# A fused attention and rational-MLP kernel: softmax sums of five early units on TensorE, fourteen rounded copies on ScalarE, a new order for the first 31 steps, and a last store in two halves

## The chip, the core and the metric

One core of one Trainium2 chip runs one program. The metric is device time in microseconds (us), the median over runs; a profiled execution gives the span, from the first to the last instruction, and a trace of every instruction. TensorE is written PE (its matmuls) and PEld (its weight loads), VectorE is DVE, ScalarE is ACT, GpSimd is POOL, and SyncE (SP) issues the transfers.

## The reference, cut to what matters

```
for c in range(seq // 32):                      # attention over chunks of 32 queries
    k_full, v_full = [mem (8 keys), k or v from 16 before to 8 after the chunk]
    scores = q_c @ k_full.T / 8
    a = exp(scores - max(scores)); a = a / (sum(a) + 1e-9)
    out_c = a @ v_full
x = out as 3072 tokens x 512                     # 4 batches x 768 tokens, 8 heads x 64
h = x @ w_in                                     # 512 x 2048
P = a0 + a1*h + a2*h**2 + a3*h**3
Q = 1 + |b0|*|h| + |b1|*h**2
y = (P / (Q + 1e-6)) @ w_out                     # 2048 x 512
```

The weights come as 64-bit floats; the kernel rebuilds each value from its two 32-bit words.

## The kernel before

**Blocks, units, steps.** The 3072 tokens are six blocks of 512. A block's attention is done in four *units* (i, p): block i, head pair p. The MLP is done in 96 *steps*, one for a block and one of 16 slices of 128 of the 2048 hidden columns. Every matrix of the MLP is split into a rounded high part and a low remainder, so that each product is three matmuls (high by high, high by low, low by high). A step n is: `g`, the first product (L477, 12 matmuls 128x512 into a PSUM bank `h`); a chain of eleven element-wise instructions on ACT, DVE and POOL; and `o`, the second product (L492, 12 matmuls into the four banks that hold a block's 512 output rows).

**The chain of a step**, with its letter: `s` |h| (L536, ACT), `S` slope (L541, ACT), `p` product for Q (L545, POOL), `i` line (L550, ACT), `j` and `J` the polynomial (L554 and L558, DVE), `t` and `T` logarithm and exponential for 1/Q (L565 and L569, ACT), `r`, `R`, `Q` ratio, error, mend (L573, L577, L581, DVE), `u` the rounded high part `ghi` (L586, POOL), `y` the low part `glo` (L593, POOL). There are two `h` banks, and 1/Q is kept in the step's own bank, so that step n+2's `g` can start only when step n's mend has read it.

**Units of blocks 0 and 1**, again with letters: `b` scores (L354, 16 matmuls 32x128), `m` and `M` maximum and subtraction (DVE), `x` exponential (ACT), `c` transposes on TensorE into a bank `ep` (L405), `k` copy of `ep` to `eT` (ACT), `d` values (L421, 16 matmuls with slices of `eT` as weights), `z` and `D` the softmax sums (DVE, L319 over 128x512 and L329), `G` reciprocal, `n` normalisation to `xt` (DVE, L432), `e` transposes back (L442), `h` and `l` high and low parts of x. Later units go through other functions.

**Weights** are converted in 32 halves, one `in` and one `out` half for each slice: `w` load, `A` (ACT, `stage`), `B` and `C` (DVE, L186 and L191), `H` high part (ACT, L198), `L` low part (POOL, L203).

**What sets the order.** `SEQ` is a list of such letters, worked off one by one; each engine keeps its instructions in that order, and SP its transfers. It holds the starting phase and the first 31 steps; `ORDER` says which weight half is converted next, `CLEAR` which engine clears which buffer at the start, `RAW_SLOTS` and `SPARE` which buffers hold raw words and spare rows. From step 31 on a loop writes the order, and `FINAL` the last steps. A capital `W` is a transpose that only keeps TensorE at work; `Y` loads the polynomial's constants `par`, and `P` takes |b| from them on ACT.

**The end.** `evac` (L525) copies each output bank through ACT to `v_main` and stores it, 256 KB for 128 rows.

Of the kernel before, what the change touches and what calls it, by code (L numbers as in the profile page):

```python
# [48 lines left out]
SEQ = """
w q00 b00 q02 A m00 q01 b02 v00 M00 m02 M02 x00 c00 q03 x02 W W b01 k00 B C W W d00 z00 D00 m01 b03 H v02 W c02 G00  # L50
M01 x01 k02 z02 m03 n00 D02 z01 w M03 d02 e00 q10 v01 A G02 c01 x03 n02 B k01 h00 C e02 b10 L l00 H D01 z03 h02 W W
d01 q11 D03 m10 c03 Y b11 M10 x10 G01 k03 v03 G03 n01 l02 z10 w e01 m11 w M11 D10 d03 h01 f00 n03 e03 w G10 A l01 B
h03 L f01 f02 x11 l03 A w f03 f10 C P q12 z11 B i f11 s j C c10 A f12 B H v10 D11 f13 S b12 A J C i L k10 w p B H t j
L C J G11 q13 T c11 m12 s d10 S r H n10 M12 R p e10 A L H t w B x12 T v11 Q w u C r b13 L h10 H l10 m13 L R k11 v12 g
M13 c12 A s i z12 w d11 Q B g j S p n11 J x13 k12 v13 C A t c13 D12 u T z13 d12 r G12 e11 k13 R H n12 s Q y D13 i d13
h11 B G13 w w e12 w C S g j A L H n13 A y B J p L h12 i t T w s l11 C S B w w H o j r l12 A R Q C u A J B H w o p B g
C u t y L T r s o R i Q S L p C g j A y A H H L B J t T w C o i r R Q s L j u S B J H C p A B t g y L T A o u s r C S
e13 R Q i j h13 p H J H l13 y B L L t g o T u C r R i Q j w J s S p A H B t g T y A C o r B R w Q s L i S C j A H H u
A J B p w w g y C t T r L i R s u S Q j o L g H J E0 p E1 B E2 t C y T L u E3 w r s R S Q w i j H p w A J t T B C o y
A r u R Q g w B o i s y L S H j A p u J t w g B y T L C C H s r R Q o i g S A p j J A H B B C o t T s r L L S i u R Q  # L60
H p A j y g J B t o T r C R s Q L i u j w S w g J H A y p o t B u C T r H w R Q i s L L A j S p J B C t g T y s i r u
R Q S y A j o C H p J g t v21 T L w B s u C y S H v20 r R o i Q p L H j u g A J A t B T B r R Q i C s L o S g j J y H
p C u t T r H o R L i Q s S L j q20 J g p y X t T o i b20 s r u j R Q J q21 m20 S p t T g M20 y i r u o R b21 x20 j s
Q S c20 w y p m21 J t M21 T g o s q22 r i z20 R x21 j d20 b22 u v22 S c21 Q J q23 D20 G20 z21 g y p o t T n20 D21 s S
r R Q u g i m22 j y o J p u G21 t T M22 x22 i r s R y j c22 S d21 b23 p Q J e20 z22 g t T o m23 r s i u S R Q M23 E0 j
E1 h20 J g n21 p t x23 y D22 T s v23 z23 S p c23 d22 r R E2 e21 Q u D23 G22 E3 i o K j y G23 g J n22 t u o q30 T r R
d23 i y l20 s Q S j h21 e22 J p g n23 t T r u s R Q o l21 y u y h22 S p g v30 i o e23 l22 j J i j t h23 T s r l23 R Q
J S o p g
# [749 lines left out]
```

## Time and profile before

| | us |
|---|---|
| median of 3 runs (lowest, highest) | 606.92 (604.62, 607.4) |
| profiled execution, its own time | 605.13 |
| its span | 603.0 |
| PE busy, of the span | 585.9 (97%) |
| DVE, ACT, POOL busy | 467.7, 396.7, 418.6 |

Busy is the time in which an engine had an instruction under way. For TensorE that says little, as matmuls overlap; how fast it can go is read where one product follows the other without a wait. What an engine waited for is in the view of waits, with the instruction that released it.

### The profile page before, as it was taken

The page shows a single profiled execution, that of the slowest core. Times are in us where ns is not written, and L with a number is a line of the kernel's source. Part 1 is how long each engine was busy: PE and PEld are TensorE (multiplying, and loading weights), DVE is VectorE, ACT ScalarE, POOL GpSimd, SP SyncE. Part 2 cuts the span into 40 slices and gives each one's busy share as a digit, 9 for nine tenths or more (in the row PEclk, how much of TensorE's full clock was granted, in tenths as well). Part 3 has the DMA queues.
Part 4 walks back from the last instruction along what each step waited for, and adds up shares of the span by engine and source line. Part 5 has one row for each costly group of instructions (what it writes and reads, how often), then busy time and mean ns, then how long its engine had stood idle before and what let it go on. Part 6 is the DMA issues. An engine that isn't in the chain of part 4 may idle for free.

```text
span 603.0 us, 12757 instructions
## 1 busy us (share of the span) xinstructions
PE 585.9 (97%) x4949; PEld 475.9 (79%) x4949; DVE 467.7 (78%) x765; ACT 396.7 (66%) x651; POOL 418.6 (69%) x388
## 2 busy tenths in 40 slices
PE   7879989999999999999999999999999999999997
PEld 6658767888778778878888888888888888888886
DVE  6999989988788758888778787787787776666673
ACT  4699879888557465565566665565756566756673
POOL 4369989999654875666685767667676767666682
PEclk9999999999999999999999999999999999999999
DMA  8968204630243704433313412312510100100001
GB/s 299 353 250 306 121 0 147 244 134 1 84 145 107 234 21 148 143 86 96 92 38 88 167 35 78 109 36 76 174 37 7 36 5 15 70 1 0 1 0 71
DMA packets 34588, 61.12 MB, mean 101 GB/s; under 512 B 4192, under 2 KB 20576, under 8 KB 34144
## 3 DMA queue, kind: packets, MB, share of 16 engines
q1 hardware_dynamic: 34528, 60.31, 30.6%
q8 instruction: 39, 0.64, 0.4%
q14 instruction: 21, 0.17, 0.1%
HBM read 44.57 MB, written 7.34 MB: 86 GB/s over the span
## 4 chain that ended last, share of the span: by engine, by line
PE 82%; DMA 5%; DVE 5%; POOL 4%; issue 2%; ACT 1%; SPq 1%; POOLq 0%; ACTq 0%; DVEq 0%
PE h L477 39%; PE o L492 38%; DMA w_raw<-in_w_dram 3%; PE pairs L312 2%; PE pairs L290 2%; POOL w_hl L203 1%; DMA v_main<-in_vm_dram 1%; DMA xf<-blocks 1%; POOL glo L593 1%; DMA qk_pairs<-in_qk_dram 1%; PE pa L421 1%; SPq L145 1%; DVE ct L558 0%; DVE ct L573 0%; DVE ct L581 0%
## 5 line engine op out<-in xcount | busy, mean ns | idle before, releaser
L477 PE MATMUL h<-x_hi,w_hl 128*128 128x512 f32 x768 | 240.6, 394 | 2.0 <-DVE ct L581 1.7
L492 PE MATMUL o<-w_hl,ghi 128*128 128x512 f32 x768 | 236.9, 390 | 0.0
L545 POOL TENSOR_TENSOR cy<-cy,ha 128x512 f32<-128x512 f32 x96 | 124.5, 1297 | 131.8 <-ACT cy L541 118.9
L477 PEld LDWEIGHTS h<-x_hi,w_hl 128*128 128x128 f32 x768 | 141.7, 188 | 34.9 <-DVE ct L581 3.4
L492 PEld LDWEIGHTS o<-w_hl,ghi 128*128 128x128 f32 x768 | 144.0, 188 | 29.9 <-POOL w_hl L203 0.2
L492 PE MATMUL o<-w_hl,glo 128*128 128x512 f32 x384 | 150.0, 391 | 1.8 <-POOL glo L593 1.8
L477 PE MATMUL h<-x_lo,w_hl 128*128 128x512 f32 x384 | 149.9, 390 | 0.0
L593 POOL TENSOR_TENSOR glo<-ct,ghi 128x512 fp32r<-128x512 f32 x95 | 122.8, 1292 | 6.2
L586 POOL TENSOR_TENSOR ghi<-ct,zero 128x512 fp32r<-128x512 f32 x95 | 98.9, 1041 | 4.3 <-PE o L492 3.1
L573 DVE SCALAR_TENSOR_TENSOR ct<-ct,par,h 128x512 f32<-128x512 f32 x82 | 61.1, 746 | 51.6 <-ACT h L569 51.3
L554 DVE TENSOR_TENSOR ct<-ct,h 128x512 f32<-128x512 f32 x96 | 65.7, 684 | 45.4 <-ACT ct L550 42.4
L565 ACT ACTIVATE h<-cy 128x512 f32<-128x512 f32 x82 | 49.2, 600 | 75.9 <-DVE ct L558 68.0
L536 ACT ACTIVATE ha<-h 128x512 f32<-128x512 f32 x96 | 57.3, 597 | 59.9 <-PE h L477 56.3
L492 PEld LDWEIGHTS o<-w_hl,glo 128*128 128x128 f32 x384 | 72.1, 188 | 18.5 <-POOL glo L593 3.4
L477 PEld LDWEIGHTS h<-x_lo,w_hl 128*128 128x128 f32 x384 | 72.1, 188 | 15.5
L541 ACT ACTIVATE cy<-ha,bab 128x512 f32<-128x512 f32 x96 | 78.5, 818 | 2.8
L550 ACT ACTIVATE ct<-h,par 128x512 f32<-128x512 f32 x96 | 73.4, 766 | 2.3 <-PE h L477 2.3
L558 DVE SCALAR_TENSOR_TENSOR ct<-ct,par,h 128x512 f32<-128x512 f32 x96 | 71.6, 746 | 2.9
L581 DVE SCALAR_TENSOR_TENSOR ct<-h,ct 128x512 f32<-128x512 f32 x82 | 56.5, 689 | 2.6
L577 DVE SCALAR_TENSOR_TENSOR h<-cy,h 128x512 f32<-128x512 f32 x82 | 56.4, 688 | 0.0
L569 ACT ACTIVATE h<-h 128x512 f32<-128x512 f32 x82 | 47.7, 582 | 2.5
L203 POOL TENSOR_TENSOR w_hl<-w_raw,w_hl 128x512 fp32r<-128x512 f32 x32 | 41.9, 1318 | 4.0 <-ACT w_hl L198 4.0
(72 smaller groups left out, 451.4 us busy)
## 6 DMA issues: line engine op xcount, KB each, us to landing
w_raw<-in_w_dram SPq DMA_DIRECT2D x26, 512.0 KB, 6.5
qk_pairs<-in_qk_dram SPq DMA_DIRECT2D x16, 576.0 KB, 3.9
...
```

What stands on the lines that cost most here:

```text
L477: pin(nc.tensor.matmul(h, lhsT=wt[:, cols], rhs=xt[i][:, ct, :], start=ct == m == 0, stop=ct == NCT - 1 and m == 2))
L492: ins = nc.tensor.matmul(o, lhsT=gt[:, cols], rhs=wt, start=begin and m == 0, stop=end and m == 2)
L536: pin(nc.scalar.activation(c["ha"], c["h"], AF.Abs))
L541: pin(nc.scalar.activation(c["y"], c["ha"], AF.Identity, scale=B1, bias=B0))
L545: pin(nc.gpsimd.tensor_tensor(c["y"], c["y"], c.pop("ha"), op=ALU.mult))
L550: pin(nc.scalar.activation(c["t"], c["h"], AF.Identity, scale=A3, bias=A2))
L554: pin(nc.vector.tensor_tensor(t, t, h, op=ALU.mult))
L558: pin(nc.vector.scalar_tensor_tensor(t, t, A1, h, op0=ALU.add, op1=ALU.mult))
L573: pin(nc.vector.scalar_tensor_tensor(t, t, A0, r, op0=ALU.add, op1=ALU.mult))
L581: pin(nc.vector.scalar_tensor_tensor(t, r, 2.0, t, op0=ALU.subtract, op1=ALU.mult, reverse0=True))
L586: pin(nc.gpsimd.tensor_tensor(ghi, chain[z]["t"], zero.broadcast_to([P, TB]), op=ALU.add))
L593: pin(engine.tensor_tensor(glo, chain.pop(z)["t"], gh[z].bitcast(F32), op=ALU.subtract))
```

## The change

Five things are edited. `SUMS_PE` names five units whose softmax sums come from TensorE: behind the 16 value matmuls stand 16 more with the same weights and a 128x2 tile of ones (made on DVE at the start from `ident`) as moving operand, written into the bank `ep`; on DVE the reduction over 128x512 goes, and the small second reduction becomes a 128x8 addition that reads that bank. `HI_ACT` names fourteen steps whose high part is an ACT copy in place of a POOL addition. `SEQ`, `ORDER`, `CLEAR`, `RAW_SLOTS` and `SPARE` are new lists. The last bank is evacuated in two halves, one by ACT with its store issued from ACT's queue, one by DVE with its store from SP's.

```diff
-HI_ACT = []
+SUMS_PE = [(0, 0), (0, 2), (1, 0), (1, 1), (1, 2)]
+HI_ACT = [3, 4, 6, 10, 11, 12, 13, 15, 17, 18, 20, 22, 23, 25]
...
-ORDER = "i0 i1 o0 o1 i2 i3 i4 i5 o2 o3 i6 o4 i7 o6 o5 i11 o7 o11 i8 i13 o13 i10 o10 i12 o12 o8 i9 o9 i14 o14 i15 o15"
+ORDER = "i0 o0 i1 i3 i2 i4 o1 i5 o2 o3 i6 i7 o4 o5 i8 o6 o7 o8 i12 i10 o10 o12 i13 o13 i9 o9 i11 o11 i14 o14 i15 o15"
...
-w q00 b00 q02 A m00 q01 b02 v00 M00 m02 M02 x00 c00 q03 x02 W W b01 k00 B C W W d00 z00 D00 m01 b03 H v02 W c02 G00
...
+w q00 Y b00 m00 q02 P A q01 M00 b02 v00 x00 B C q03 m02 w v02 c00 W W b01 m01 M02 H k00 W W d00 D00 b03 v01 w x02 M01
...
+    ones = const.tile([P, 2], F32, name="ones")
...
     def att_sums(i, p):
         u = unit[i, p]
+        if (i, p) in SUMS_PE:
+            return
...
-        if i < BLOCKWISE:
+        if (i, p) in SUMS_PE:
+            pin(nc.vector.tensor_scalar(rinv, u["ep"][:, :2 * NG], 1e-9, None, op0=ALU.add))
+        elif i < BLOCKWISE:
             pin(nc.vector.tensor_reduce(rinv, sums, axis=AX.X, op=ALU.add))
...
+        if (i, p) in SUMS_PE:
+            sv = u["ep"][:, :2 * NG].rearrange("x (g h) -> x g h", h=2)
+            for g, j, c in places(i):
+                pin(nc.tensor.matmul(sv[j * CHUNK:(j + 1) * CHUNK, g], lhsT=u["eT"][:, c * CHUNK:(c + 1) * CHUNK], rhs=ones,
+                                     start=True, stop=True, tile_position=(0, j * CHUNK)))
...
+            if (i, t) == (NBLK - 1, NG - 1):
+                y, rows = stage(), slice(i * TB + t * P, i * TB + (t + 1) * P)
+                for cols, queue in ((slice(0, DM // 2), nc.scalar), (slice(DM // 2, DM), nc.sync)):
+                    if queue is nc.scalar:
+                        pin(nc.scalar.mul(y[:, cols], o[:, cols], 1.0 / W_SCALE))
+                    else:
+                        pin(nc.vector.tensor_scalar(y[:, cols], o[:, cols], 1.0 / W_SCALE, None, op0=ALU.mult))
+                    load(out[rows, cols], y[:, cols], queue)
+                continue
...
+        if SUMS_PE:
+            pin(nc.vector.tensor_reduce(ones, ident.rearrange("p (w h) -> p h w", h=2), axis=AX.X, op=ALU.max))
```

Three places in the instructions' order show what the lists move. Line numbers of the changed kernel are higher by one to twenty: L332 is its small addition, L432 its sums, L487 and L502 are `g` and `o`, L592, L596 and L600 are `r`, `R`, `Q`, L605 and L612 are `ghi` and `glo`.

The first is DVE ahead of the mend of step 0, which stands in the last row; `xt` is the normalised tile of unit (0, 3). Before:

```order
L554 TENSOR_TENSOR ct<-ct,h 128x512
L191 SCALAR_TENSOR_TENSOR w_raw<-w_raw,stage 128x512
L558 SCALAR_TENSOR_TENSOR ct<-ct,par,h 128x512
L335 RECIPROCAL rinv<-rinv 128x8
L362 TENSOR_REDUCE mx<-pa 128x8
L573 SCALAR_TENSOR_TENSOR ct<-ct,par,h 128x512
L432 SCALAR_TENSOR_TENSOR xt<-pa,rinv 128x512
L372 TENSOR_TENSOR e<-pa,mx 128x4x2x64
L577 SCALAR_TENSOR_TENSOR h<-cy,h 128x512
L186 TENSOR_SCALAR stage<-stage 128x512
L581 SCALAR_TENSOR_TENSOR ct<-h,ct 128x512
```

Now, from step 0's own `j` to its mend:

```order
L573 TENSOR_TENSOR ct<-ct,h 128x512
L577 SCALAR_TENSOR_TENSOR ct<-ct,par,h 128x512
L367 TENSOR_REDUCE mx<-pa 128x8
L377 TENSOR_TENSOR e<-pa,mx 128x4x2x64
L367 TENSOR_REDUCE mx<-pa 128x8
L592 SCALAR_TENSOR_TENSOR ct<-ct,par,h 128x512
L377 TENSOR_TENSOR e<-pa,mx 128x4x2x64
L596 SCALAR_TENSOR_TENSOR h<-cy,h 128x512
L332 TENSOR_SCALAR rinv<-pa 128x8
L600 SCALAR_TENSOR_TENSOR ct<-h,ct 128x512
```

Unit (0, 3)'s `xt` and step 1's `j` and `J` no longer stand ahead of the mend; the small addition that reads the sums of unit (1, 0) from TensorE does.

The second is TensorE's start, the units of block 0, with `pa` for every bank. Before:

```order
L642 MATMUL warm<-ident 128x128 x2
L421 MATMUL pa<-v_main_101,eT 32x128 x16
L354 MATMUL pa<-qk 32x128 x16
L642 MATMUL warm<-ident 128x128
L405 MATMUL pa<-ident,e 128x128 x4
L421 MATMUL pa<-v_first,eT 32x128 x16
```

Now:

```order
L661 MATMUL warm<-ident 128x128 x2
L426 MATMUL pa<-v_main_102,eT 32x128 x16
L432 MATMUL pa<-ones,eT 32x2 x16
L359 MATMUL pa<-qk 32x128 x16
L661 MATMUL warm<-ident 128x128
L410 MATMUL pa<-ident,e 128x128 x8
L452 MATMUL pa<-ident,xt 128x128 x4
L426 MATMUL pa<-v_first,eT 32x128 x16
L432 MATMUL pa<-ones,eT 32x2 x16
```

Sixteen matmuls of two columns follow the values of a unit in `SUMS_PE`, and two units' transposes stand together ahead of the second unit's values.

The third is POOL from the high part of step 2 on. Before:

```order
L586 TENSOR_TENSOR ghi<-ct,zero 128x512
L545 TENSOR_TENSOR cy<-cy,ha 128x512
L586 TENSOR_TENSOR ghi<-ct,zero 128x512
L593 TENSOR_TENSOR glo<-ct,ghi 128x512
L203 TENSOR_TENSOR w_hl<-w_raw,w_hl 128x512 x2
L545 TENSOR_TENSOR cy<-cy,ha 128x512
L593 TENSOR_TENSOR glo<-ct,ghi 128x512
L203 TENSOR_TENSOR w_hl<-w_raw,w_hl 128x512 x2
L586 TENSOR_TENSOR ghi<-ct,zero 128x512
L545 TENSOR_TENSOR cy<-cy,ha 128x512
L593 TENSOR_TENSOR glo<-ct,ghi 128x512
```

Now:

```order
L605 TENSOR_TENSOR ghi<-ct,zero 128x512
L564 TENSOR_TENSOR cy<-cy,ha 128x512
L204 TENSOR_TENSOR w_hl<-w_raw,w_hl 128x512
L612 TENSOR_TENSOR glo<-ct,ghi 128x512
L390 MEMSET e 32x16
L390 MEMSET e 32x32
L204 TENSOR_TENSOR w_hl<-w_raw,w_hl 128x512 x2
L564 TENSOR_TENSOR cy<-cy,ha 128x512
L612 TENSOR_TENSOR glo<-ct,ghi 128x512
```

The second `glo` here, that of step 3, has no `ghi` ahead of it on POOL any more: it is one of the fourteen.

SP's list changes too: the load of `par` stood behind 16 other transfers of the start and stands now behind three, ahead of the second unit's `qk`.

## Rows read from the trace of the kernel before

**Rows 1.** The page's head: the span, and TensorE's busy time and instructions.

```profile
span 603.0 us, 12757 instructions
...
PE 585.9 (97%) x4949; PEld 475.9 (79%) x4949; DVE 467.7 (78%) x765; ACT 396.7 (66%) x651; POOL 418.6 (69%) x388
```

**Rows 2.** The chain that ended last, once TensorE no longer waits.

```profile
97.53 2.72 PE h L477 x12
```

**Rows 3.** Engines' busy time by stretch: length, PE, PEld, DVE, ACT, POOL, then clock, DMA.

```profile
10.00:41.66 31.66, 25.27 (x436) 18.82 (x428) 29.78 (x59) 22.82 (x41) 12.46 (x18) 1.00 0.83 301
...
91.75:599.30 507.55, 506.22 (x4148) 413.36 (x4148) 388.24 (x627) 325.96 (x532) 353.99 (x313) 1.00 0.26 79
...
91.75:150.00 58.25, 58.25 (x257) 48.20 (x258) 52.46 (x81) 50.03 (x85) 56.69 (x48) 1.00 0.38 135
```

**Rows 4.** TensorE's waits, 6 to 92 us: who for whom, total, times, longest.

```profile
PE pa L442 <- DVE xt L432: 3.2, 2, 3.0
...
PE o L492 <- POOL glo L593: 1.8, 1, 1.8
PE h L477 <- DVE ct L581: 1.1, 2, 0.8
PE pa L421 <- ACT eT L412: 0.7, 1, 0.7
PE pa L405 <- POOL e L385: 0.6, 1, 0.6
PE pa L421 <- issue: 0.5, 1, 0.5
PE pa L405 <- DVE rinv L335: 0.5, 1, 0.5
```

**Rows 5.** TensorE in order of time: start, us, instruction, idle before it.

```profile
39.17 0.66 PE L442 MATMUL pa<-ident,xt 128*128 128x128 f32 x4 [2.98 <-DVE xt L432]
...
41.66 0.71 PE L477 MATMUL h<-x_hi,w_hl 128*128 128x512 f32 x2 [0.76 <-DVE ct L581]
```

**Rows 6.** DVE in order of time, ahead of the first mend.

```profile
38.44 0.68 DVE L432 SCALAR_TENSOR_TENSOR xt<-pa,rinv 128x512 f32<-128x512 f32 x1
39.04 0.68 DVE L372 TENSOR_TENSOR e<-pa,mx 128x512 f32<-128x512 f32 x1
```

**Rows 7.** POOL in order of time, the longest wait after 41 us.

```profile
86.46 1.28 POOL L545 TENSOR_TENSOR cy<-cy,ha 128x512 f32<-128x512 f32 x1 [2.97 <-ACT cy L541]
```

**Rows 8.** Groups by line and shape: busy us, mean ns, idle before.

```profile
L586 POOL TENSOR_TENSOR ghi<-ct,zero 128x512 fp32r<-128x512 f32 x95 | 98.9, 1041 | 4.3 <-PE o L492 3.1 <-DVE ct L581 0.5
...
L304 DVE TENSOR_TENSOR e<-pairs,mx 128x256 f32<-128x256 f32 x32 | 12.0, 416 | 0.4
...
L319 DVE TENSOR_REDUCE sums<-e 128x8 f32<-128x512 f32 x8 | 5.5, 681 | 0.6 <-POOL e L385 0.2
...
L588 ACT CAST ghi<-ct 128x512 fp32r<-128x512 f32 x1 | 0.6, 624 | 2.6 <-PE o L492 2.6
```

**Rows 9.** TensorE in order of time, two groups of small matmuls.

```profile
13.12 1.08 PE L421 MATMUL pa<-v_main,eT 128*32 128x128 f32 x32
...
171.81 0.86 PE L290 MATMUL pairs<-qk_pairs 64*32 64x64 f32 x64 [0.61 <-DMA qk_pairs<-in_qk_dram]
```

**Rows 10.** SP's queue in order of time: start, us, transfers issued.

```profile
1.57 4.46 SPq L145 DMA_DIRECT2D qk<-in_qk_dram  x6
...
14.77 1.29 SPq L145 DMA_DIRECT2D par<-in_ab_dram  x1
```

**Rows 11.** Transfers by tile: size, median us from issue to landing.

```profile
par<-in_ab_dram SPq DMA_DIRECT2D x1, 3.0 KB, 6.1
```

**Rows 12.** ACT in order of time: the first exponential of a unit.

```profile
10.09 0.63 ACT L389 ACTIVATE e<-e 128x512 f32<-128x512 f32 x1 [4.91 <-DVE e L372]
```

**Rows 13.** The chain that ended last: its end.

```profile
599.34 0.60 ACT v_main L525
```

More of the change, by code (lines that the diff above doesn't have):

```diff
@@ L35 @@
 X_SLOTS = [0, 1, 1, 0, 1, 0]
-HI_ACT = []
+SUMS_PE = [(0, 0), (0, 2), (1, 0), (1, 1), (1, 2)]
+HI_ACT = [3, 4, 6, 10, 11, 12, 13, 15, 17, 18, 20, 22, 23, 25]
 XL_POOL = [(0, 0), (0, 2), (1, 0), (1, 1), (1, 2)]
 WARM = 14
-CLEAR = [("qk", 2, "pp"), ("v", 2, "pa"), ("v", 1, "pa"), ("qk", 0, "vv"), ("qk", 1, "pa"), ("v", 3, "pv"), ("v", 0, "vp"), ("qk", 3, "pv")]
+CLEAR = [("qk", 0, "vp"), ("qk", 3, "ap"), ("qk", 1, "pv"), ("qk", 2, "vv"), ("v", 1, "pa"), ("v", 2, "pv"), ("v", 0, "pp"), ("v", 3, "pp")]
 LEAD = 22
@@ L46 @@
 XB = {"xf": 2, "eT": 2}
-ORDER = "i0 i1 o0 o1 i2 i3 i4 i5 o2 o3 i6 o4 i7 o6 o5 i11 o7 o11 i8 i13 o13 i10 o10 i12 o12 o8 i9 o9 i14 o14 i15 o15"
+ORDER = "i0 o0 i1 i3 i2 i4 o1 i5 o2 o3 i6 i7 o4 o5 i8 o6 o7 o8 i12 i10 o10 o12 i13 o13 i9 o9 i11 o11 i14 o14 i15 o15"
 V_SLOTS = [10, 11]
 SEQ = """
-w q00 b00 q02 A m00 q01 b02 v00 M00 m02 M02 x00 c00 q03 x02 W W b01 k00 B C W W d00 z00 D00 m01 b03 H v02 W c02 G00
-M01 x01 k02 z02 m03 n00 D02 z01 w M03 d02 e00 q10 v01 A G02 c01 x03 n02 B k01 h00 C e02 b10 L l00 H D01 z03 h02 W W
@@ L52 @@
[L52 to L66, printed above, removed]
@@ L67 @@
-d23 i y l20 s Q S j h21 e22 J p g n23 t T r u s R Q o l21 y u y h22 S p g v30 i o e23 l22 j J i j t h23 T s r l23 R Q
-J S o p g
+w q00 Y b00 m00 q02 P A q01 M00 b02 v00 x00 B C q03 m02 w v02 c00 W W b01 m01 M02 H k00 W W d00 D00 b03 v01 w x02 M01
+q10 G00 n00 x01 m03 W c02 c01 M03 e00 A k02 B d02 z01 D02 k01 h00 v03 L x03 A D01 G02 n02 G01 W W d01 w w e02 z03 c03
+l00 n01 C h02 f00 e01 B D03 h01 q11 k03 b10 q12 C v10 l01 H L G03 d03 m10 l02 n03 f01 H e03 f02 A M10 B L h03 x10 l03
+A C B f03 f10 w f11 w C s b11 i j J c10 S m11 p H k10 b12 t f12 T v11 f13 L H M11 x11 m12 r d10 M12 s R D10 A L w i Q
@@ new lines @@
+B S j p v12 G10 c11 g k11 x12 A J d11 c12 C t T u B i s k12 n10 r D11 R j G11 S y p e10 w Q u h10 J d12 q13 A t C T B
+n11 D12 r G12 H R g A i s e11 n12 H l10 b13 S Q e12 L L w B y m13 h12 C h11 M13 g A i o p j H J C w j B o t w T s L r
+u H C R S Q J A w p B A B g L y o u w t T H x13 C H c13 L i C L r R A s Q S B g k13 j H p z13 J y A C D13 t B T l11 u
+C i H r w o L L R Q A w s B j w C J v13 G13 S p d13 H y g A n13 t T u l12 B w e13 s S h13 r i R H p o C Q j J l13 A t
+L y T L B r C R g H s i o Q S u A L j J H B w A B w p t T g y L s o C S i H r R w u Q C j g y A p w w J H A B w L t T
@@ new lines @@
+u y r i R s Q o E0 S E1 w j J E2 g E3 p t w T B i L C C r R Q s H S j o u A J p y A t T L B B g H r s R i S L C A Q j
+J u o p u B y t T g y C r R s i Q S A w j H o w J g u p H L t T s S i C B p r A R Q j H w J t T o L y g s L S B i C o
+p u w r C A R Q j A H J B t T y B u C r g y L R i A s Q S j p B o g H J L H C u t T y s i C S H r R Q p L A o j J g t
+T i u w L s S o B r R Q C A p j J u B t v20 g T H H A r y R L L s S Q o C H p B C y i g u j i L X J t y T v21 H L j o
+s r R Q S J q20 o p u t T r R g i y Q u b20 s j g S o m20 J i q21 y M20 p j b21 t x20 s T S p z20 J r R Q q22 t T c20
@@ L69 @@
+m21 M21 D20 r u o x21 R g s Q y z21 i S b22 u m22 p q23 c21 D21 g j J M22 G20 t T o r i s R x22 Q j J S d20 b23 p u t
+y v22 T c22 g o n20 r R q30 Q s i g m23 S j J p t y T s o u M23 z22 i d21 y G21 r E0 R x23 e20 S D22 Q p E1 E2 j J t u
+T r v23 g y i s n21 E3 R S p Q j e21 o J t d22 u z23 c23 T g G22 r D23 i s R h20 S h21 Q y o j J p g t T s l20 v30 u
+G23 n22 o r R i Q d23 y S j l21 e22 J w g p t s T u n23 h22 e23 r y R S l22 K o p h23 o i l23 Q j g J
 """
@@ L76 @@
 """
-RAW_SLOTS = [8, 16, 6, 13, 8, 9, 11, 15, 16, 14, 15, 12, 9, 14, 15, 16]
-SPARE = 9
+RAW_SLOTS = [4, 9, 8, 7, 16, 13, 9, 11, 14, 16, 13, 14, 15, 9, 15, 16]
+SPARE = 14
 def start_of(c):
@@ L411, in att_keep @@
         eT = u["eT"] = room(at, "eT", F32, "eT", 2)
-        pin(nc.scalar.copy(eT, u.pop("ep")))
+        pin(nc.scalar.copy(eT, u["ep"]))
     def att_values(i, p):
```

## The prediction, made before the run

> **What bounds the kernel now.** I read the page's head first: TensorE is busy for 585.9 of 603.0 us, DVE for 78%, POOL for 69% [rows 1]. Busy does not say that it runs at its pace, so the chain that ended last comes next: from 92 us on it is one product after the other, 12 matmuls in 2.72 us each [rows 2], and to 599.30 us TensorE is busy for 506.22 of 507.55 us [rows 3]. There the time is TensorE's own work, 5.44 us a step, and nothing that the change does on other engines can shorten it. What can be won lies in the first 92 us, where TensorE's waits are the view to read [rows 4]. Without the wait of the first scores for their data, they sum to 3.2 + 1.8 + 1.1 + 0.7 + 0.6 + 0.5 + 0.5 = 8.4 us. These split into two kinds.
>
> *Late waits, 5.9 us.* At 39.17 TensorE had waited 2.98 us for the normalised tile of unit (0, 3), and at 41.66 another 0.76 for the mend of step 0 [rows 5]; both stand in DVE's queue, which between 10 and 41.66 us was busy for 29.78 of 31.66 us and issues a full-width instruction every 0.60 us (38.44, 39.04) [rows 3, 6]. The mends' total is 1.1 [rows 4]. Late in the stretch TensorE waits 1.8 us for POOL's low part of step 6; just ahead of it POOL had itself stood 2.97 us for a slope from ACT [rows 4, 7]. So 3.0 + 1.1 + 1.8 = 5.9.
>
> *Early small waits, 2.5 us.* The other 0.2 for a normalised tile, then 0.7, 0.6, 0.5, 0.5: attention of block 0, where each operation needs the one before it on another engine.
>
> **The change, part by part.**
>
> *DVE's queue ahead of the first mend.* By the order of instructions, from the first maximum to step 0's mend DVE has ten full-width instructions fewer: four sums, two `B`, one `C`, one `xt`, and step 1's `j` and `J`. At 0.60 us that is 6.0 us, more than the 2.98 + 0.76 that TensorE waited behind that queue. Also, unit (0, 3)'s `xt` now stands ahead of step 0's chain. I take the 3.0 and the 1.1 as gone. What is late next: the mend stands directly behind the addition that reads unit (1, 0)'s sums, so `g` of step 2 now needs TensorE's own sums, which stand before it on TensorE. As these come one transpose group ahead of that `g`, I price this wait at nothing; if that cover is missing, one DVE operation of 0.68 [rows 6] shows.
>
> *DVE's work.* Five sums of 681 ns leave it [rows 8], 3.4 us; this pays only through the waits above, since DVE is not waited for after 92 us for longer than the 1.3 us that TensorE idles there in all [rows 3].
>
> *TensorE's work.* Five times 16 matmuls of two columns are added, and TensorE cannot hide them where it has no waits left. The trace has none with two columns. From above: the values, same weights and positions with 128 columns, take 1.08 us for 16, which the trace shows as 32 records, two for each. From below: 64 records (32 matmuls) with 64 columns take 0.86 us, so 16 matmuls take 0.43 [rows 9]. That is 2.1 to 5.4 us for five units. Two columns are nearer to 64 than to 128, so I take 0.5 us a unit, 2.5 us.
>
> The 64 records of rows 9 start 13 ns apart, the 32 matmuls 27 ns. The Trainium skill, "TensorE: Matmul & The Clock Gate", section "Wait — 56ns, not 53.3ns?", says that start to start never falls below about 25 ns however few the columns. Counted for each record that rule gives an estimate of 0.8 us a unit, 4.0 in all, and my sum would lose 1.5 of its gain; the 13 ns speak against it. Counted for each matmul it gives 0.4 us, 2.0 in all, 0.5 more gain, and the 27 ns bear it out.
>
> *High parts.* Fourteen additions of 1041 ns leave POOL and fourteen copies of 624 ns come to ACT [rows 8]: 14.6 us off, 8.7 us on. Up to the low part of step 6, three of POOL's seven `ghi` are gone, 3.1 us, more than the 1.8 that TensorE waited for it. POOL was busy for 56.69 of 58.25 us from 91.75 on, ACT for 50.03 [rows 3], so the move also takes the fuller engine's load. On ACT I price the copies at nothing: eight of the fourteen steps fall into that stretch (10 to 20), 5.0 us into 8.2 us that are free. What that costs if they come at the wrong place is a rival below.
>
> *The start.* The load of `par` moves ahead of the second unit's keys, and takes 1.29 us of SP's time [rows 10]. The second unit's scores are next in TensorE's queue, so the first transposes behind them come later by at most that; I take 0.8. It lands 6.1 us after its issue [rows 11]; |b| waits for it on ACT, the first weight half's `A` is queued behind that, and then the first exponential. Behind two `qk` loads (six take 4.46 us from 1.57 on [rows 10]) it is issued near 3.1 and lands near 9.2. The first exponential ran at 10.09 [rows 12], and `A` takes no longer than it (0.63), so this fits by some 0.3 us. In `SEQ` the low part of x of unit (0, 2) stands behind a weight's low part on POOL, which waits for its own high part on ACT: one POOL operation of 1.3 us, of which I take half, 0.6. On the other side, the transposes of two units standing together fill the time in which `eT` is copied (0.7), and the other three small waits (1.2) have other work ahead of them. So 1.4 is new against 1.9 gone at best, and the sums lengthen a unit's chain. I leave the early kind at 2.5 us, with 1.4 either way as its bounds.
>
> *The end.* After the last matmul at 599.34 come 0.60 us of copy and then 3.06 us to the end of the span [rows 1, 13]. Half the columns on DVE take 416 ns against ACT's 600 for all [rows 8, 13], 0.2 us; the same bytes go out, through two queues. I take 0.3, between 0 (the halves queue behind each other) and 0.8 (half of the store's wait for what stood ahead of it as well).
>
> **The sum.** -5.9 late waits, +2.5 sums, 0 early, -0.3 end: -3.7 us. The profiled execution took 605.13, 2.13 more than its span, so 601.4 in its terms. The median of the runs is 606.92; the shift applied to it is **603.2 us**, and that is the forecast. Its own range is 601.4 to 605.0: sums from 2.1 to 2.9, early waits 1.4 either way. A change of 0.5%, 3.0 us, is about what a measurement of this kernel can tell from none.
>
> **The rivals.**
>
> 1. *Everything fits.* The early waits go too (2.5), sums cost 2.1, the end gives 0.8: -5.9 - 2.5 + 2.1 - 0.8 = -7.1, 599.8 us. For it: POOL and DVE both lose work at each of the waits. Against it: the operations of one unit depend on each other across four engines, and five units have one exchange more. Chance 0.13.
>
> 2. *DVE waits for the sums instead.* Each addition of L332 stands in DVE's queue in front of full-width work, and the sums reach it only after the exponential, the transposes, the copy on ACT and the values. If DVE stands 0.9 us at each, 4.5 us, it loses more than the 3.4 it was spared, and the 4.1 us behind its queue stay. Left are -1.8 + 2.5 - 0.3 = +0.4: 607.3 us. Behind a waiting addition stand the next unit's subtraction, so ACT's exponential, and in step 0 the mend, so `g` of step 2. Chance 0.17.
>
> 3. *Sums as dear as values.* The cost is 5.4 instead of 2.5: -0.8, 606.1 us. For it: the weights are the same, and their loads may set the pace. Against it: the 27 ns a matmul of the pairs, which load weights for each as well [rows 9]. Chance 0.10. By the floor in the Trainium skill's page, above, counted for each record, the estimate would lie between, at 604.7.
>
> 4. *ACT becomes the bound, and the kernel slower.* With 5.0 us more, ACT is at 55.0 of 58.25 us from 91.75 on, and the copies stand among logarithms and exponentials on which DVE's next three operations wait. A step's `g` starts after the mend of two steps before; if each of the fourteen steps came 0.6 us late at it, +8.4 - 3.7 = +4.7, 611.6 us. It turns slower than before from 0.26 us a step on (3.7 over 14). Against it: of 58.25 us ACT had 8.2 free, and TensorE had no wait there though POOL had only 1.6 free. Chance 0.10.
>
> **How the numbers follow.** The forecast has 0.50. Faster by over 0.5% needs more than 3.0 us of gain: about 0.35 of the forecast's 0.50, and all of rival 1, 0.48. Within 0.5%: the other 0.15, rival 3 (0.10), most of rival 2 (0.13): 0.38. Slower by more: rival 4 and the rest of 2, 0.14. The range reaches from rival 1 to a little above rival 2, 599.6 to 607.4; outside it are rival 4 and what lies beyond rivals 1 and 2.
>
> **What would show it.** TensorE's waits up to the eleventh `g`: none above 1 us on L442, L487 or L502, where 2.98, 0.76 and 1.8 stood; the stretch in which it no longer waits begins near 88.4 (91.75 - 5.9 + 2.5) instead of 91.75. The group of L432: 16 matmuls in about 0.5 us. DVE's idle time before L332: below 0.9 us each. POOL's `ghi` 81, ACT's 15. From 92 to 150 TensorE without waits on L600. Wrong would be: a wait on L600 or L607 past 92 us (rival 4), L332 with over 4 us of idle time in total (rival 2), the first exponential more than 1 us later than at 10.09 (the load of `par`).

## The result, and the profile after

The changed kernel takes 600.12 us (median of 5 runs, 599.85 to 601.09) where before took 606.92: a ratio of 0.9897 [0.9862, 0.9931], 1.0% faster. The forecast was 603.2, its range 599.6 to 607.4. The time lies in the range that was put around forecast and rivals, but outside the forecast's own range (601.4 to 605.0) and 0.3 us from the 599.8 of rival 1. The profiled execution took 600.12 too, 5.01 less than that of before (605.13); the spans differ by 4.8. That the medians differ by 6.8 needs an explanation of its own, below.

The page's head after, to be held against [rows 1]:

```profile
span 598.2 us, 13082 instructions
...
PE 587.6 (98%) x5109; PEld 478.6 (80%) x5109; DVE 464.9 (78%) x762; ACT 401.8 (67%) x664; POOL 406.4 (68%) x375
```

TensorE has 160 more records and is busy 1.7 us longer, in a span that is 4.8 us shorter. Its waits to 92 us after (who for whom, total, times, longest), against [rows 4]:

```profile
PE pa L359 <- DMA qk<-in_qk_dram: 3.2, 2, 2.8
...
PE pa L359 <- issue: 0.7, 1, 0.7
PE pa L426 <- ACT eT L417: 0.6, 2, 0.4
PE h L487 <- DVE ct L600: 0.3, 1, 0.3
PE pa L410 <- POOL e L390: 0.3, 1, 0.3
```

The wait of 3.0 on `xt` and that of 1.8 on `glo` are gone, the mends' 1.1 are 0.3. New is that the second unit's scores wait 0.4 for keys (3.2 less the 2.8 of the first). TensorE in order of time after, the first scores and the eleventh `g`:

```profile
7.51 1.93 PE L359 MATMUL pa<-qk 128*32 128x128 f32 x32 [2.82 <-DMA qk<-in_qk_dram]
...
88.28 0.61 PE L487 MATMUL h<-x_hi,w_hl 128*128 128x512 f32 x2
```

and the engines' busy time from there on (columns as in [rows 3]):

```profile
88.28:594.51 506.23, 506.04 (x4149) 413.11 (x4147) 387.53 (x627) 330.74 (x543) 343.03 (x302) 1.00 0.25 76
...
91.75:150.00 58.25, 58.25 (x259) 48.18 (x258) 51.61 (x80) 51.98 (x88) 48.86 (x40) 1.00 0.32 109
```

The eleventh `g` starts 3.47 us earlier (91.75 before). From it to the last matmul's end pass 506.23 us instead of 507.55, as TensorE's idle time there fell from 1.33 to 0.19. Both together are the 4.8 us: what lies behind the last matmul is 3.69 us after and 3.70 before.

### The profile page after: what moved, and what is told of

It is laid out like the page before. It is cut to its first block, busy times and chain, and to the rows that moved or that the text cites. A ratio compares the mean times of both kernels' runs of the same rounds, so it can differ in the third digit from the quotient of the medians.

```text
span 598.2 us, 13082 instructions
## 1 busy us (share of the span) xinstructions
PE 587.6 (98%) x5109; PEld 478.6 (80%) x5109; DVE 464.9 (78%) x762; ACT 401.8 (67%) x664; POOL 406.4 (68%) x375
## 4 chain that ended last, share of the span: by engine, by line
PE 93%; DVE 2%; DMA 1%; ACT 1%; issue 1%; SPq 1%; POOL 1%; POOLq 0%; DVEq 0%
PE h L487 43%; PE o L502 42%; PE pairs L313 2%; PE pairs L291 2%; PE pa L426 1%; PE pa L359 1%; DMA qk<-in_qk_dram 1%; SPq L146 1%; PE pa L410 1%; PE pa L452 1%; DMA xf<-blocks 1%; DVE qk L220 0%; PE pa L432 0%; ACT eT L417 0%; ACT cy L560 0%
## 5 line engine op out<-in xcount | busy, mean ns | idle before, releaser
L487 PE MATMUL h<-x_hi,w_hl 128*128 128x512 f32 x768 | 240.6, 395 | 0.4 <-DVE ct L600 0.3
L502 PE MATMUL o<-w_hl,ghi 128*128 128x512 f32 x768 | 236.9, 390 | 0.0
L502 PEld LDWEIGHTS o<-w_hl,ghi 128*128 128x128 f32 x768 | 143.9, 188 | 29.8 <-ACT v_main L544 0.2
L487 PEld LDWEIGHTS h<-x_hi,w_hl 128*128 128x128 f32 x768 | 141.6, 188 | 32.5 <-DVE ct L600 1.1
L502 PE MATMUL o<-w_hl,glo 128*128 128x512 f32 x384 | 150.0, 391 | 0.1
L487 PE MATMUL h<-x_lo,w_hl 128*128 128x512 f32 x384 | 149.7, 390 | 0.0
L612 POOL TENSOR_TENSOR glo<-ct,ghi 128x512 fp32r<-128x512 f32 x95 | 122.9, 1294 | 9.1 <-ACT ghi L607 3.2
L592 DVE SCALAR_TENSOR_TENSOR ct<-ct,par,h 128x512 f32<-128x512 f32 x82 | 61.2, 746 | 55.8 <-ACT h L588 55.3
L605 POOL TENSOR_TENSOR ghi<-ct,zero 128x512 fp32r<-128x512 f32 x81 | 84.4, 1041 | 2.8 <-PE o L502 1.2
L502 PEld LDWEIGHTS o<-w_hl,glo 128*128 128x128 f32 x384 | 72.1, 188 | 16.9 <-POOL glo L612 1.7
L487 PEld LDWEIGHTS h<-x_lo,w_hl 128*128 128x128 f32 x384 | 72.1, 188 | 15.9 <-DVE x_lo L468 0.4
L600 DVE SCALAR_TENSOR_TENSOR ct<-h,ct 128x512 f32<-128x512 f32 x82 | 56.5, 689 | 2.6
L596 DVE SCALAR_TENSOR_TENSOR h<-cy,h 128x512 f32<-128x512 f32 x82 | 56.5, 689 | 0.0
```

The costliest lines, as they stand in the source:

```text
L487: pin(nc.tensor.matmul(h, lhsT=wt[:, cols], rhs=xt[i][:, ct, :], start=ct == m == 0, stop=ct == NCT - 1 and m == 2))
L502: ins = nc.tensor.matmul(o, lhsT=gt[:, cols], rhs=wt, start=begin and m == 0, stop=end and m == 2)
L592: pin(nc.vector.scalar_tensor_tensor(t, t, A0, r, op0=ALU.add, op1=ALU.mult))
L596: pin(nc.vector.scalar_tensor_tensor(r, yy, QC, r, op0=ALU.add, op1=ALU.mult))
L605: pin(nc.gpsimd.tensor_tensor(ghi, chain[z]["t"], zero.broadcast_to([P, TB]), op=ALU.add))
L612: pin(engine.tensor_tensor(glo, chain.pop(z)["t"], gh[z].bitcast(F32), op=ALU.subtract))
```

## The experiments

Twelve kernels were run, in three groups. The time of before is measured beside each again. Where the time goes is seen best at two marks, read by counting the records of `g` in each trace: the 121st (the eleventh step's first) and the 240th (the end of twenty steps' `g`), in us from the span's start, to within 0.02. The twelfth record, the last of step 0's `g`, stands beside them: the first high part that was moved to ACT runs at 58.7 us in the changed kernel, so a difference at the twelfth record is not the high parts'.

| kernel | 12th | 121st | 240th | span |
|---|---|---|---|---|
| before | 29.80 | 91.77 | 143.38 | 603.0 |
| after | 30.27 | 88.30 | 139.77 | 598.2 |
| no_hi | 30.88 | 90.48 | 145.06 | 604.1 |
| hi_early | 29.93 | 87.89 | 141.95 | 601.2 |
| hi_late | 30.55 | 90.06 | 142.13 | 600.4 |
| no_sums | 29.99 | 89.01 | 140.52 | 598.6 |
| old_hi | 29.28 | 92.17 | 144.50 | 604.7 |
| par_late | 28.66 | 86.68 | 138.20 | 596.4 |
| warm25 | 32.97 | 90.93 | 142.43 | 600.6 |
| par_warm | 32.25 | 90.29 | 141.78 | 600.2 |

### Parts undone in the changed kernel

```diff
 no_hi:    -HI_ACT = [3, 4, 6, 10, 11, 12, 13, 15, 17, 18, 20, 22, 23, 25]
           +HI_ACT = []
 no_sums:  -SUMS_PE = [(0, 0), (0, 2), (1, 0), (1, 1), (1, 2)]
           +SUMS_PE = []        # and z of these units behind their c in SEQ
 lists_alone:  both of these
 one_store: the last bank leaves as all others do
```

Without the sums on TensorE, the one tile of sums is overwritten by the next unit before some units read it.

**no_hi.** Expected:

> The changed kernel with all high parts back on POOL, everything else as changed. Theory A (POOL's queue was the second thing TensorE waited for): POOL carries 3.1 us more by the low part of step 6 and 14.6 us more by step 25; TensorE waits on L502 for POOL's low part again, 1 to 2 us in all before 92 us and some more up to 150: 601 to 604 us. Theory B (lists alone): POOL has enough slack in the new order, within 0.5 us of the changed kernel's 600.1.

Measured: 606.05 us, 0.9987 [0.9973, 1.0001] of before. That is above both theories. The high parts are worth 5.9 us in the new order by the medians. By the marks 0.6 us are lost ahead of the twelfth record, which is not the high parts' doing (in this execution the granted clock stood at 0.50, its level of 1.2 GHz, from 10 to 15 us, in the changed kernel's at 1.00). Theirs are 1.6 from there to the eleventh `g`, 3.1 more to the 240th record and 0.6 behind it. In the trace TensorE waits for POOL again, on both sides of 88 us (three of its rows in order of time):

```profile
88.04 0.51 PE L502 MATMUL o<-w_hl,glo 128*128 128x512 f32 x1 [0.31 <-POOL glo L612]
...
111.60 0.50 PE L502 MATMUL o<-w_hl,glo 128*128 128x512 f32 x1 [0.94 <-POOL glo L612]
...
131.77 0.50 PE L487 MATMUL h<-x_hi,w_hl 128*128 128x512 f32 x1 [0.49 <-POOL w_hl L204]
```

**no_sums.** Expected:

> The changed kernel with all five units' sums back on DVE (the reduction stands right behind each unit's transposes in the list), everything else as changed. Theory A (DVE's queue ahead of the first mends held TensorE, so sums on TensorE pay): DVE gets back 5 x 0.6 = 3.0 us ahead of the first mends and loses its 1.3 us of waits for TensorE's sums; TensorE loses 1.7 us of work (five groups of 0.28 to 0.49 us in the chain after) but waits about 2 to 4 us more for normalised tiles or mends before 60 us: 600.5 to 602.5 us against the changed kernel's 600.1. Theory B (the new lists alone do it, the sums only add work to TensorE): 598.4 us, no new waits.

Measured: 600.88 us (599.88 to 601.13), 0.9896 [0.9875, 0.9918]. No difference to the changed kernel can be told (0.7 us at the last two marks). TensorE is spared 1.7 us of sums, and waits 1.7 us for mends, which DVE now does later, where the changed kernel waits 0.3; up to 92 us its waits, without that of the first scores, sum to 4.6 instead of 2.3:

```profile
PE h L491 <- DVE ct L604: 1.7, 2, 0.9
PE pa L430 <- ACT eT L421: 1.1, 2, 0.9
```

**lists_alone.** Expected:

> The changed kernel with sums on DVE and high parts on POOL: only the lists (order of steps, conversions, clears, slots) and the split last store are new. Theory A: the two costs of the two undone parts add up, 602 to 606 us, TensorE's waits both on mends and on low parts. Theory B: 598.4 to 600.5 us, as fast as the whole change or faster by the 1.7 us of sums that TensorE is spared.

Measured: 605.77 us, 0.9978 [0.9963, 0.9992]. The new order alone takes away the wait of 2.98 on `xt` (0.3 is left), with the sums back on DVE, and others come in its place (TensorE's waits):

```profile
PE h L491 <- DVE ct L604: 2.1, 4, 0.9
...
PE o L506 <- POOL glo L616: 1.2, 2, 0.9
PE pa L430 <- ACT eT L421: 1.1, 2, 0.9
PE h L491 <- POOL w_hl L208: 0.8, 2, 0.5
```

**one_store.** Expected:

> The changed kernel with the last bank leaving in one piece through ACT and one store. In the profile after, DVE's half starts only when ACT's half has ended (594.53 + 0.38, then 594.95), and from the last matmul's end to the end of the span it is 3.7 us, as before the change. Theory A (the split is worth nothing because the halves follow each other): within 0.2 us of the changed kernel, 3.7 us after the last matmul. Theory B (it is worth the 0.3 us of the prediction): 0.3 us slower, 4.0 us after the last matmul.

Measured: 601.05 us, 0.9903 [0.9882, 0.9924], no difference that can be told. TensorE's last matmul ends at 595.05 and the span at 598.7, 3.65 us later, as with two halves. The two halves show why, in the changed kernel's trace, ACT's and DVE's rows:

```profile
594.53 0.38 ACT L534 ACTIVATE v_main<-o 128x256 f32<-128x256 f32 x1
...
594.95 0.42 DVE L536 TENSOR_SCALAR v_main<-o 128x256 f32<-128x256 f32 x1 [4.73 <-ACT v_main L534]
```

DVE's half starts when ACT's ends: 0.38 + 0.42 take longer than the 0.60 of the whole. The Trainium skill, "PSUM — Partial Sum Buffer", section "PSUM bank collisions raise a hardware error", says that the compiler's scheduler adds a dependency between instructions of two engines that touch the same bank and the same 32 partitions, reads too. The row agrees in that DVE was released by ACT; but the halves also share the tile `v_main`, and no run tells bank and tile apart.

**Which of the fourteen.** Steps 3, 4 and 6 alone, or the eleven later ones alone:

```diff
 hi_early: +HI_ACT = [3, 4, 6]
 hi_late:  +HI_ACT = [10, 11, 12, 13, 15, 17, 18, 20, 22, 23, 25]
```

Expected of the early three:

> The changed kernel with only the high parts of steps 3, 4 and 6 on ScalarE, those of the eleven later steps on GpSimd again. Without all fourteen TensorE stood idle 4.6 us instead of 2.5 between 7.5 and 88.28 us, and 1.8 instead of 0 between 88.28 and 150. Theory, each stretch loses to its own steps: the first stretch stays as in the changed kernel, the second loses 1.8 us, so 601.5 to 602.5, with a wait on glo or ct past 88 us. Rival, the eleven late ones carry nearly all: 604.5 to 606. Second rival, the three early ones carry all, since GpSimd gets ahead by them once: 600 to 601.

Measured: 603.27 us, 0.9930 [0.9904, 0.9957]. Expected of the late eleven:

> The changed kernel with only the eleven high parts of step 10 and later on ScalarE. Theory, each stretch loses to its own steps: the eleventh g starts about 2 us later than 88.28, nothing is lost behind it, so 602 to 603. Rival, the eleven late ones carry nearly all: 600 to 601. Second rival, the three early ones carry all: 605 to 606, with waits on glo on both sides of 88 us.

Measured: 602.44 us, 0.9915 [0.9891, 0.9939]. The late eleven lie in the range of their theory, the early three 0.8 above theirs. Each stretch loses to its own steps, though not by what TensorE's waits say. From the twelfth record to the eleventh `g` pass 58.0 us in the changed kernel and with the early three, 59.5 with the late eleven and 59.6 with none: the early three are worth 1.5 there. From the eleventh `g` to the 240th record pass 51.5 us in the changed kernel, 52.1 with the late eleven, 54.1 with the early three and 54.6 with none: the late eleven are worth 2.6 there, and 0.8 more behind it (span less 240th). In the second stretch TensorE's matmuls, and then its weight loads, wait with the early three:

```profile
PE o L502 <- POOL glo L612: 0.9, 1, 0.9
PE h L487 <- POOL w_hl L204: 0.5, 1, 0.5
PE h L487 <- DVE ct L600: 0.2, 1, 0.2
```

```profile
PEld o L502 <- POOL glo L612: 1.4, 1, 1.4
PEld h L487 <- POOL w_hl L204: 0.9, 1, 0.9
PEld h L487 <- DVE ct L600: 0.6, 1, 0.6
```

The same three waits are 1.6 us in the one view and 2.9 in the other, and 2.6 are lost: a matmul is 0.39 long and the next starts 0.23 behind it, so the first 0.16 of a wait lie beside the matmul before it and do not show as idle time, and the first matmul behind a wait takes 0.50 (rows of no_hi). That is 0.27 of the 0.33 a wait.

### Parts alone in the old order

```diff
 old_hi:   HI_ACT as in the change, all else as before
 old_sums: +SUMS_PE = [(0, 0), (0, 2), (1, 0), (1, 2)], with D and G behind d, and the last bank in halves; all else as before
```

**old_hi.** Expected:

> The kernel of before with the fourteen high parts moved from GpSimd to ScalarE and nothing else. In the new order taking them back cost 5.9 us (606.05 against 600.12). Theory, the order and the high parts need each other: in the old order only the waits on GpSimd's glo go (1.8 us), the waits on VectorE's xt (3.0) and ct (1.1) stay, so 604.5 to 605.5 against a median of before near 607. First rival, the high parts alone are the change: 600.5 to 602, and the waits on xt go with them. Second rival, ScalarE is late in the old order: 607 or more, with TensorE or VectorE waiting for ScalarE.

Measured: 608.03 us, 1.0005 [0.9984, 1.0026]: nothing, in the order in which they were expected to save 1.8 us. POOL, ACT and TensorE at that wait:

```profile
86.87 1.29 POOL L545 TENSOR_TENSOR cy<-cy,ha 128x512 f32<-128x512 f32 x1 [3.92 <-ACT cy L541]
```

```profile
85.34 0.60 ACT L536 ACTIVATE ha<-h 128x512 f32<-128x512 f32 x1 [2.32 <-DVE ct L558]
```

```profile
89.44 0.50 PE L492 MATMUL o<-w_hl,glo 128*128 128x512 f32 x1 [1.75 <-POOL glo L593]
```

Step 6's addition of 1.04 us is gone ahead of it and went into POOL's own idle time, 3.92 instead of 2.97 [rows 7], and TensorE waits 1.75 instead of 1.79. In the old order `glo` stands behind a product that waits for ACT's slope, so POOL's load is not what makes it late. ACT itself, ahead of that slope, had waited 2.32 us for DVE's polynomial (2.75 in before), so the second rival, a late ACT, has the time but not the cause.

**old_sums.** Expected:

> The kernel of before with the sums of four early units (five don't fit into its order of banks) taken from TensorE and nothing else changed. In the new order, without the sums 600.88 against 600.12, no difference that can be told. Theory, in the old order they cost TensorE their time, 4 times 0.35 us, and take nothing from the wait on xt (3.2 us), since that follows from VectorE's order: 607.5 to 609 against a median of before near 607. Rival, VectorE's relief shortens that wait: 604 to 606. Second rival, they fill TensorE's idle time: within 0.5 us of before.

Measured: 607.92 us, 1.0021 [1.0005, 1.0038]. TensorE, two of its rows:

```profile
17.87 1.08 PE L430 MATMUL pa<-v_first,eT 128*32 128x128 f32 x32 [1.38 <-ACT eT L421]
...
39.81 0.63 PE L456 MATMUL pa<-ident,xt 128*128 128x128 f32 x4 [3.07 <-DVE xt L446]
```

Four reductions off DVE leave the wait on `xt` where it was (3.07 against 2.98), and one on `eT` grows from 0.7 to 1.4. No part of the change gains more than 0.2% by itself: 0.9978 for the lists, 1.0005 for the high parts, 1.0021 for the sums, and 0.9897 together.

### The start, and the spread of before

**before_again.** The kernel of before, unchanged. Expected:

> The kernel of before, for a second profile. Its times spread from 604.2 to 609.1 us in one chip's runs, the changed kernel's from 599.9 to 601.1, and the profile that the prediction used (605.13) lies low in that spread, with a granted clock of 1.00 from 35 to 40 us, where TensorE is busy 1.9 of 5 us. Theory, the spread is the clock: a run of 606.5 or more shows the granted clock at 0.5 for some us behind the idle stretches near 35 or 87 us, and its waits are as before. Rival, the spread is transfers: the clock is as before, and the waits on xt or on the keys are 1 to 3 us longer.

Measured: 606.78 us, span 604.7, 1.7 more than in the first profile. TensorE in order of time, and its windows:

```profile
38.96 0.66 PE L442 MATMUL pa<-ident,xt 128*128 128x128 f32 x4 [2.98 <-DVE xt L432]
40.60 1.94 PE L354 MATMUL pa<-qk 128*32 128x128 f32 x32 [0.99 <-DMA qk<-in_qk_dram]
42.47 1.22 PE L477 MATMUL h<-x_hi,w_hl 128*128 128x512 f32 x2
```

```profile
40.00:42.00 2.00, 1.40 (x28) 1.43 (x32) 2.00 (x5) 2.00 (x5) 1.73 (x4) 0.50 1.02 399
42.00:44.00 2.00, 2.00 (x16) 1.33 (x9) 1.95 (x4) 2.00 (x5) 2.00 (x3) 0.50 1.03 414
44.00:46.00 2.00, 2.00 (x6) 1.57 (x5) 2.00 (x4) 0.25 (x1) 2.00 (x2) 0.50 0.74 295
```

Behind the wait of 2.98 the granted clock stands at 0.50, that is 1.2 GHz, for some 6 us. The same two matmuls of `g` take 1.22 us here and 0.71 in the first profile [rows 5]; in 44 to 46 us six records fit. From the twelfth to the 60th record of `g` pass 28.22 us instead of 25.35, of which 0.99 is the wait for keys. So the late `xt` costs its 3 us and, in such a run, some 2 more. Behind the same wait the clock is down in the traces of old_hi (0.53 over 38 to 40 us, 0.62 over 40 to 42) and old_sums (0.80, 0.50 and 0.84 over 40 to 46) as well, so it fell in three of four executions, and the first profile is the exception. Over all 70 runs of before that stood beside these kernels, the 7 with a mean granted clock of 0.998 or more have a median of 604.41 us, the other 63 of 607.09; but two of the seven stand at 607.1, so the clock is not all of the spread. The five of the changed kernel have 0.997 to 1.0.

**par_late.** The load of `par` behind the next block's keys again:

```diff
-w q00 Y b00 m00 q02 P A q01 ...
+w q00 b00 m00 q02 A q01 ... q10 Y ...      # and P ahead of the first S
```

Expected:

> The changed kernel with the small load of the parameters issued where the old order had it, behind the keys of the next block, and the work that waits for it moved behind it. In the changed kernel this load stands between the second and the third load of keys, takes 0.58 us of the queue, and the first scores start 0.87 us later than before (7.51 against 6.64). Theory, the load ahead of the keys is what made them late: first scores near 6.7, time 599.3 to 599.9. Rival, the late start is hidden or comes from the other transfers: 599.9 to 600.6, scores still near 7.5. Second rival, what waits for the parameters is now late: 601 or more, a wait of TensorE behind ScalarE's part of the first steps.

Measured: 598.42 us (598.23 to 600.62), 0.9875 [0.9852, 0.9898], the best of all and below every theory. TensorE's first scores, and its eleventh `g` 1.62 us earlier than at 88.28:

```profile
6.91 3.64 PE L363 MATMUL pa<-qk 128*32 128x128 f32 x64 [2.21 <-DMA qk<-in_qk_dram]
...
86.66 0.61 PE L491 MATMUL h<-x_hi,w_hl 128*128 128x512 f32 x2
```

Both units' scores now follow each other. What the load delays is the second unit's: they start at 9.76 to 10.23 us in the seven traces with the early load and 14 warm-ups, and at 8.31 to 8.61 in the five with the late one (before, before_again, old_hi, old_sums, par_late; in before the load stood behind 20 transfers, not 16). The start of the first unit's goes from 6.57 to 7.97 in kernels that start alike, so the 7.51 against 6.64 is not the load's. The gain is there by the twelfth record (1.6 us), 0.67 of it a gap of the changed kernel's that is told of below. The intervals of the two ratios overlap; the 1.62 us at the eleventh `g` and the 1.8 between the spans say the same as the medians (1.7).

**warm25** and **par_warm.** More warm-up transposes, so that TensorE does not stand idle ahead of the first scores: 25 in the changed kernel, 27 in par_late, instead of 14. Expected of the first:

> The changed kernel with 25 instead of 14 warm-up transposes. In the changed kernel the 14 end at 4.69 us, the first scores start at 7.51 and take 1.93 us; in two other kernels of this study, which idled there too, the granted clock showed 0.5 from about 10 to 15 us. 25 of them end near 7.3. Theory, the idle time costs little, since what follows waits for the keys and their transfers: 599.8 to 600.5, first scores still near 7.5. Rival, the idle time makes the early units slow: the first scores take 1.1 instead of 1.9 us and the time is 598.5 to 599.5. Second rival, the added transposes run into the first scores: 600.5 to 601.

Measured: 602.52 us, 0.9914 [0.9890, 0.9938], slower than any theory had it. Expected of the second, given that:

> The version with the late parameter load (598.42 us, ratio 0.9875 to before) with 27 instead of 14 warm-up transposes, which should end near 6.6 us, just ahead of its first scores at 6.91. There the first two scores took 3.64 us behind an idle time of 2.2; with 25 warm-ups in the changed kernel one took 1.08 instead of 1.93, but TensorE then stood 2.02 and 1.95 us at two places for nothing that the profile shows, and the time was 602.52. Theory, these gaps belong to the added instructions and come again: 599.5 to 601.5, with gaps without a releaser of 3 us or more by 30 us. Rival, they belong to the early load in that order: no such gap above 0.7 us, the early scores at 1.08, 596.9 to 597.9. Second rival, the faster start is lost in the next wait for transfers or sums: 598.1 to 598.8.

Measured: 602.42 us, 0.9934 [0.9908, 0.9960], 4 us more than par_late and above every theory, though the gaps of the first came. TensorE with 25 warm-ups:

```profile
6.76 1.08 PE L359 MATMUL pa<-qk 128*32 128x128 f32 x32 [0.45 <-POOL v_main L220]
...
17.40 0.42 PE L359 MATMUL pa<-qk 128*32 128x128 f32 x5 [2.02 <-issue]
...
25.54 0.40 PE L487 MATMUL h<-x_hi,w_hl 128*128 128x512 f32 x1 [1.95 <-issue]
...
27.08 1.94 PE L359 MATMUL pa<-qk 128*32 128x128 f32 x32
```

and with 27:

```profile
16.38 0.42 PE L363 MATMUL pa<-qk 128*32 128x128 f32 x7 [1.58 <-issue]
...
24.50 0.27 PE L414 MATMUL pa<-ident,e 128*128 128x128 f32 x1 [2.27 <-issue]
```

The first scores do take 1.08 instead of 1.93 us. Then TensorE stands twice, with no releaser in the profile, and behind the second gap the granted clock is down (0.66 and 0.67 over 25 to 30 us), where scores take 1.94 and 1.91. What these gaps are is told first by counting: PE's and PEld's records up to the start of each gap, with 25 and then with 27 warm-ups, and to the changed kernel's one gap of 0.67 at 25.49:

```profile
0.00:15.40 15.40, 11.50 (x220) 10.02 (x220) 8.99 (x16) 6.20 (x10) 8.15 (x20) 1.00 0.81 284
0.00:23.57 23.57, 17.51 (x345) 15.02 (x346) 14.68 (x29) 11.07 (x19) 10.87 (x24) 1.00 0.89 328
```

```profile
0.00:14.79 14.79, 11.21 (x220) 9.65 (x220) 8.75 (x16) 6.02 (x8) 8.16 (x20) 1.00 0.86 310
0.00:22.20 22.20, 16.89 (x345) 14.40 (x346) 14.21 (x28) 10.55 (x17) 10.89 (x24) 1.00 0.91 336
```

```profile
0.00:24.83 24.83, 19.33 (x345) 15.82 (x345) 15.75 (x31) 11.84 (x20) 10.87 (x24) 1.00 0.91 334
```

The gaps lie behind the 220th and the 345th matmul, whatever these are and whenever they come. No_hi, hi_early, hi_late and one_store, which start as the changed kernel does, have the one at the 345th too (0.39 to 0.91 us).

The traces also hold, one by one, the packets of the queue that the changed kernel's page lists as this (number, MB, share of 16 engines):

```profile
q8 instruction: 40, 0.66, 0.5%
```

The first two of these packets behind the start, 16 KB each, end at 15.85 and 23.94 us with 25 warm-ups and at 15.01 and 23.05 with 27, and TensorE goes on 1.54 and 1.60, then 1.37 and 1.45 us later; in the changed kernel the second ends at 24.12, 1.37 ahead of 25.49. In none of the 14 traces does the matmul behind the 220th start sooner than 1.3 us after the end of the first packet, nor the one behind the 345th sooner than 1.2 after that of the second. So the gaps read as waits for TensorE's next instructions. The packets bear no engine's name, but with 160 more matmul records and as many weight loads there are 40 of them instead of 39. With 25 warm-ups the 220th record is over at 15.4 us, where the changed kernel goes past it at 18.1; the first packet ends only 0.7 us sooner (15.85, 16.57). Why it lands no sooner, beside transfers that keep the DMA engines busy for 0.91 of this time, was not tried.

The 4 us split by operation. The last transposes ahead of the first `g` start at 21.73 with 27 warm-ups and at 21.74 in par_late: the first gap has eaten what the faster start gave. The first `g` starts at 24.52 instead of 22.10, 2.4 us late by the second gap, and the twelfth record is 3.6 us late (32.25, 28.66), the last 1.2 of it where the clock is down.

## Why the prediction was right, and where it was off

**The mechanism.** The late waits went (5.9 to 0.3 us), and the stretch without waits starts at 88.28 against the forecast's 88.4. That is errors that nearly cancel: the sums came 0.8 cheaper, the start 0.4 dearer, and 0.3 of the late waits stayed, so that the terms below add up to -3.5 for this stretch against the forecast's -3.4.

**Sums on TensorE, +2.5 forecast, +1.7 measured.** This term was mis-sized, and its lower bound (2.1) did not hold. Sums of a unit in the changed kernel, 32 records:

```profile
15.49 0.45 PE L432 MATMUL pa<-ones,eT 128*32 128x2 f32 x32
```

One record is 0.17 long, and the group starts that much ahead of the values' end (14.59 + 1.08 = 15.67); along the chain that ended last the five groups take 0.49, 0.30, 0.35, 0.28 and 0.28. The pairs' 64 columns were no bound from below for two. From record to record it is (0.45 - 0.17) / 31 = 9 ns, 18 a matmul, so the floor of 25 ns in the Trainium skill, "TensorE: Matmul & The Clock Gate", section "Wait — 56ns, not 53.3ns?", does not show for these, counted either way; they go in turn to four column positions, and what those have to do with it was not tried. Rival 3 falls. DVE waited for the sums, in this view of the changed kernel, at most:

```profile
16.24 0.17 DVE L332 TENSOR_SCALAR rinv<-pa 128x8 f32<-128x8 f32 x1 [0.59 <-PE pa L432]
```

1.3 us in all, three times: rival 2 (4.5) falls. But the term's other side was missing: the sums buy back the 2.3 us that no_sums waits longer, 1.4 of them for mends, so by themselves they are worth nothing that can be told.

**Early small waits, 0 forecast.** The waits are 0.4 + 0.7 + 0.6 + 0.3 = 2.0 instead of 2.5, and the first scores come 0.87 us later: +0.4, inside the ±1.4. The load of `par` was priced at 0.8 for the first transposes behind the second unit's scores, and it did about that: they run at 11.82 us, 10.94 in before, 11.21 in par_late. It took 0.58 of SP's time instead of the 1.29 read. Its offset by other savings is what failed, as par_late shows by gaining 1.7 without it. Among the small waits that other work was to fill is the 0.5 without a releaser, which came again as 0.7; by the packets above it reads as a wait for instructions. The first exponential ran at 10.96, 0.87 later than in [rows 12]; |b| had its constants at 7.88, so not by them.

**DVE's queue.** The order took the 3.0 with it, as the lists alone show. There three of the four sums, of the ten instructions counted, are back on DVE ahead of that mend, and the wait is gone all the same; so they were not needed for it. But DVE's relief without the order (old_sums) takes nothing from that wait.

**High parts.** The step that failed is this term's reason: "three of POOL's seven `ghi` are gone, 3.1 us, more than the 1.8 that TensorE waited". The same text had read that POOL itself stood 2.97 us for ACT ahead of that `glo`; a queue that waits is not made earlier by less work, and old_hi shows it. The 1.8 was the order's to remove: in no_hi, with all high parts on POOL, 0.3 of it is left ahead of 92 us. And the new order needs the high parts: without them it loses 1.6 us to the eleventh `g` and 3.1 and more behind it. The forecast counted the early three alone and gave the eleven late ones nothing, as TensorE did not wait there before; they keep 2.6 us that the new order would otherwise lose. Rival 4 falls: in 91.75 to 150 ACT is busy 51.98 of 58.25 us, and TensorE all of it.

**Past 92 us.** The idle 1.33 us there, 0.6 for a mend and 0.6 for keys, was read and put in no term; 1.1 of it went.

**The end, -0.3 forecast, 0 measured.** That the halves queue behind each other was the bound given for 0; the place is the copies, where DVE is released by ACT, not the stores.

**The sum.** Late waits -5.6, sums +1.7, early +0.4, past 92 us -1.1, end 0: -4.6 of the 4.8 by which the spans differ. The forecast's -3.7 was 1.1 short. Of the other 2.0 us of the miss, 1.8 are the shift by 1.79 us from the profiled execution to the median. It took for a constant what is, as far as before_again shows it, the fallen clock behind the `xt` wait, which that profile happened not to have; with the wait, the clock's fall goes too, and the changed kernel's profile and median agree. That the shift is the clock alone is not shown (two of the seven runs above). The last 0.2 is a run's own time less its span, 2.13 before and 1.92 after. Rival 1 had the time, 599.8, but not the terms: its 2.5 of early waits are still 2.0, and of its 0.8 at the end nothing came. That the result lies in the whole range is owed to that rival's number, and so in part to luck.
